# q and k of the last batch transposed by DMA instead of by TensorE, loads of batches 2 and 3 gated four deep, and a new order of issue

## The chip, the cores and the metric

The kernel runs on one core of one Trainium2 chip. The metric is the device time of one execution in microseconds (us). A core has TensorE (PE in the profile; its weight loads are PEld), VectorE (DVE), ScalarE (ACT), GpSimd (POOL) and SyncE (SP), each with its own stream of instructions taken in order, and 16 DMA engines. SBUF is the on-chip memory, PSUM the memory that TensorE writes.

## The reference

An attention with a narrow window feeds a mixing layer. Four batches, 8 heads, 768 positions, head size 64; 512 channels.

```python
# attention: q, k, v are (4, 8, 768, 64); n_global = 8, n_local = 96
scores = scale * np.matmul(q, k.transpose(0, 1, 3, 2))
rel = pos[:, None] - pos[None, :]
keep = (pos[None, :] < n_global) | ((rel >= 0) & (rel < n_local))
scores = scores + (-slopes[:, None, None] * dist[None, :, :])[None]
a = softmax(np.where(keep, scores, -1e9))
x = np.matmul(a, v)            # then (batch, position, 512 channels)
# mixing layer
theta = x @ w_theta
zr, zi = x * np.cos(theta), x * np.sin(theta)
y = einsum('ts,bsd->btd', w_tok_r, zr) + einsum('ts,bsd->btd', w_tok_i, zi)
u = x + y
out = u + np.maximum(u @ w_ch, 0.0)
```

## The kernel before

**Tiling.** A batch's 768 positions are six tiles of 128, taken in three groups `g` of two. Because a query sees 96 positions back and the first 8, a group needs score blocks with its own two key tiles and the last one of the group before. The first 8 keys and values are put in place of the first 8 rows of a tile's copy (`kp`, `kg` in `twin`; `vpa`, `vpb` in `vprev`).

**Names.** Each piece of work has a name with the digits batch, group (or tile), part. For a batch `b`: `load` brings q, k (both as bf16, lines 240 to 251) and v from DRAM through GpSimd's queue; `t{b}{g}{i}0` transposes q (`i` = 0) or k (`i` = 1) of a group on TensorE, eight blocks of 128x128, into PSUM (line 425), and `q{b}{g}0` or `k{b}{g}0` copies the result to SBUF, to the tile `qT` or `kk` (line 439). `kk` has room for each key block twice; the second copy is made by `kp` (line 384) and `kg` (line 388). `s{b}{g}{p}` makes the scores of two heads (line 499), `x` their exponentials on ScalarE (line 526), `m` the multiplication with the table of biases (line 534), `v` the product with the values (line 556), `n` the division (lines 567, 569), which fills the tile `x`. `xt` transposes that tile: on TensorE for batches 0 and 1, by a DMA transpose issued from SP for batches 2 and 3 (line 589). `th` multiplies with w_theta (line 601), `cos` and `sin` run on ScalarE (lines 610, 612), `z` multiplies on VectorE (line 622). `mx{b}{tile}{g}` mixes positions (line 644); `u` adds (line 656); `ut` transposes u, from batch 1 on by a DMA transpose issued from SP (line 676, except the very last tile); `ch` multiplies with w_ch (line 688); `o` makes the output tile on VectorE (line 694); `st` stores it from SP (line 704). `ts` and `tx` load ScalarE's tables for sine and for exponentials (lines 733, 713).

**Stages.** While the mixes and channel products of one batch fill TensorE, the attention of the next runs in between; the mixes of a batch need the `z` of all its groups.

**What sets the order.** All instructions are issued in the order of the text `ORDER` (lines 37 to 92), one global list by name; every engine takes its own part of it in that order. A suffix `/ACT` or `/DVE` picks the engine, `+n` puts n filler matmuls before the operation (`fill`, line 142). The numbers that the `add` calls carry (costs, priorities) aren't used here: `Plan.add` (line 23) keeps name, engine and function. Waits between engines follow from which tiles an instruction reads and writes.

**Buffers.** Tiles of a kind share a fixed number of buffers (line 124): a new tile takes one that is free when everything that used its last tile is done. Those that matter here are the output tiles `o` (3), `qT` and `kk` (3 each), `cs`, the pair of cosine and sine (3), and `pa` and `pb`, the PSUM tiles (4 each).

```python
bufs = dict(qk=6, qT=3, kk=3, e=8, x=8, xT=3, zri=5, cs=3, u=4, uT=3, o=3, w_nat=7, pa=4, pb=4)
```

**Loads.** There are 82, numbered in the order of issue: 47 to 64 are batch 2's, 65 to 82 batch 3's. From load 20 on, each has a gate: a copy of one element on GpSimd that reads what load `n - depth` brought (line 234), so that load `n` isn't issued before that one has landed. The depth is `DEPTH1` = 8 up to load 46 and `DEPTH` = 6 from load 47 on.

**The switch.** `trans_qk` holds a second path that the kernel before does not take, since `TQ` is empty: for the groups listed in `TQ` the transposition is one DMA transpose, issued from SP, straight from the loaded tile to `qT` or to every other block of `kk` (lines 398 to 408), without the copy from PSUM.

Of the kernel before, what the change touches and what calls it, by code (L numbers as in the profile page):

```python
# [15 lines left out]
class Plan:  # L16
# [6 lines left out]
    def add(self, name, eng, fn, **_):  # L23
        op = self.ops[name] = SimpleNamespace(name=name, fn=fn, took=next(iter(eng)))
        return op
# [12 lines left out]
zero hw00 hw10 halfpi rel ones2 ones1 hw01 warm0 ones0 hw11 ones5 ones3 ones6 ones4 load1 tiny sid4 sid3 sid7  # L38
sid1 sid0 sid2 load2 sid5 sid6 ident far0 far1 load3 dtab0 dtab1 dtab2 load4 cast00/ACT dtab3 bi0000+1
cast10/DVE etab5 bi0001 t0000 load5 t0010 q000/ACT bi0010 bi0011 k000/DVE load6 etab7 kg000 cast01/DVE etab4  # L40
load7 kp000/DVE t0001+22 cast11/DVE etab1 s001 q001/DVE t0011 load8 etab0 s000 k001/DVE x0000 load9 kg001
x0001 kp001/DVE t0100+14 etab6 bi0020 load10 bi0021 q010/DVE x0010 t0110 x0011 s002 load11 k010/DVE etab2
bi0030 bi0031 s003 kp010/DVE x0020 load12 x0021 vpa00/DVE bi0100+2 x0030 kg010 vpb00/DVE bi0101+1 load13 x0031
s010 etab3 v000 v002 load14 v001 n000 x0100 bi0110 bi0111 vpa01/DVE s011 x0101 load15 vpb01/DVE bi0120 x0110
v003 n002 bi0121 load16 s012 x0111 n003 bi0130 load17 x0120 v010 n001 bi0131 s013 x0121 load18 n010 bi0200
x0130 v012 load19 v011 x0131 n012 t0200 gate20 t0210 n011 q020/ACT load20 v013 k020/DVE xt00 gate21 bi0201
kg020 xc00/ACT bi0210 kp020/DVE load21 bi0211 vpa02/DVE s020+1 n013 s021 gate22 x0200 vpb02/DVE load22 xt01+6
x0201 bi0220 x0210 xc01/DVE v020+1 bi0221 x0211 gate23 n020 bi0230 load23 s022 bi0231 x0220 s023 gate24 tw00
x0230 load24 th001 twc00/DVE x0231 gate25 x0221 v021 load25 v023 n021 ts0 tw10 gate26 v022 load26 twc10/DVE
th000 n023 gate27 tw11 n022 cos000 load27 th010 twc11/DVE sin000 xt02 gate28 cos001 z000 load28 tw01 sin001  # L50
th011 xc02/DVE gate29 cos010 z001 load29 th020 sin010 twc01/DVE gate30 cos011 load30 th021 z010 sin011 gate31
cos020 t1000 load31 z011 tw20 sin020 q100/DVE tw21 cos021 gate32 mx000 z020 load32 twc20/ACT twc21/DVE mx001
gate33 sin021 vpa10/DVE load33 tx1 vpb10/DVE t1010 z021 mx020 gate34 k100/DVE load34 mx002 kp100/DVE gate35
kg100 mx022 load35 u00 gate36 s100 load36 s101 ut00 x1000 mx021 gate37 x1010 uc00/DVE load37 x1001 tw31 x1011
u02 tw30 twc31/ACT gate38 s102 m100 load38 s103 t1100 x1020 m101 x1030 mx010 gate39 q110/DVE x1031 load39
x1021 v100 m103 mx012 twc30/ACT m102 gate40 load40 n100 tw40 v102 twc40/DVE mx011 gate41 n102 load41 t1110 u01
tw41 gate42 v103 k110/DVE load42 twc41/ACT ut01 ut02 v101 kg110 uc02/DVE ch00 uc01/ACT gate43 kp110/DVE load43
vpa11/DVE ch01 n103 gate44 load44 vpb11/DVE s110 n101 t1200 gate45 x1100 o00 load45 ch02 x1101 q120/DVE st00
t1210 gate46 o01 load46 s111 k120/DVE s112 st01 x1110 mx030 gate47 kp120/DVE x1120 load47 o02 mx032 x1121
kg120 gate48 x1111 m110 st02 mx031 load48 m111 s113 gate49 u03 s120 load49 x1130 tw50 m112 tw51 twc50/ACT v110  # L60
gate50 twc51/DVE xt10 load50 x1131 n110 mx040 vpa12/ACT xc10/DVE gate51 mx042 load51 m113 x1200 mx041
vpb12/DVE x1201 gate52 load52 m120 v111 mx050 n111 gate53 load53 u04 s121 v120 x1210 v113 gate54 n120 ut03
load54 x1211 mx052 n113 uc03/ACT gate55 m121 mx051 load55 vpa20/DVE s122 u05 gate56 s123 x1220 ch03 load56
vpb20/DVE x1221 ut04 x1230 gate57 o03 ut05 v121 load57 uc04/ACT v112 n121 th100 st03 uc05/ACT gate58 n112
x1231 load58 ch04 m122 ts1 m123 gate59 xt11 load59 v122 xc11/DVE cos100 v123 th101 gate60 n122 sin100 load60
n123 ch05 cos101 o04 gate61 sin101 xt12 load61 o05 st04 th110 xc12/ACT vpa21/DVE gate62 st05 z100 th111 load62
cos110 z101 sin110 th120 gate63 vpb21/DVE load63 cos111 z110 th121 sin111 gate64 cos120 load64 t2110 z111
sin120 t2010 k210/DVE gate65 cos121 t2200 load65 z120 mx100 k200/ACT kp210/DVE gate66 q220/DVE mx101 sin121
load66 kp200/DVE tx2 t2000 z121 gate67 mx120 kg210 load67 vpa22/DVE q200/DVE mx102 gate68 vpb22/DVE load68
kg200 mx110 u10 gate69 s200 load69 ut10 s201 mx111 x2000 x2001 gate70 x2010 mx121 load70 m200 x2011 v200 m201  # L70
gate71 mx112 load71 n200 s202 u11 gate72 s203 t2100 x2020 load72 x2021 mx122 ut11 q210/DVE x2030 gate73 x2031
m202 t2210 load73 u12 s210 k220/ACT s211 gate74 vpa30/DVE ut12 ch10 load74 vpb30/DVE x2100 kp220/DVE x2101
mx130 gate75 o10 load75 x2110 m210 s212 x2111 st10 mx131 gate76 m203 x2120 load76 m211 x2121 v210 mx132 n210
gate77 load77 m212 v201 s213 n201 ch11 gate78 x2130 load78 kg220 u13 x2131 v202 s220 n202 gate79 ut13 v203
load79 mx140 x2200 m213 x2201 n203 s221 gate80 load80 v212 vpa31/DVE x2210 xt20 mx142 m220 x2211 gate81 n212
s222 load81 v220 vpb31/DVE x2220 v213 n220 mx141 gate82 x2221 load82 n213 v211 m222 s223 ch12 n211 x2230 x2231
m221 v222 xt21 mx150 ts2 m223 v221 n222 v223 mx151 n221 n223 th200 o12 xt22 th201 o11 cos200 vpa32/DVE sin200
mx152 st11 u14 cos201 st12 vpb32/DVE ch13 sin201 ut14 u15 z200 th210 ut15 o13 th211 cos210 z201 sin210 st13
th221 cos211 z210 t3000 sin211 t3010 q300/DVE t3110 k300/DVE t3210 th220 k310/DVE k320/ACT kp300/DVE t3100
z211 cos220 mx200 kg300 q310/DVE sin220 mx201 cos221 kg310 kp310/DVE kg320 sin221 kp320/DVE t3200 z220 tx3  # L80
ch15 q320/DVE z221 s300 s301 mx220 x3000 o15 x3001 x3010 mx202 st15 m300 x3011 s302 m301 s303 mx222 u20 x3020
x3021 x3030 ut20 v300 m302 mx221 x3031 n300 v302 m303 ch14 n302 s310 o14 s311 x3100 mx210 u22 st14 x3110 v303
x3111 ut22 mx212 n303 x3101 m311 mx211 m310 v301 ch20 u21 n301 ut21 mx230 o20 s312 st20 s313 x3120 mx232 xt30
x3130 v310 x3121 ch22 n310 x3131 m312 s320 s321 o22 x3200 mx250 x3201 m313 st22 v311 x3210 mx231 n311 x3211
m320 s322 s323 u23 x3220 mx251 x3221 m321 ut23 v313 x3230 ch21 m322 x3231 n313 ts3 v312 v321 m323 mx240 n312
v320 o21 v322 xt31 mx241 n320 n321 v323 mx242 st21 n323 n322 th300 u24 xt32 mx252 cos300 sin300 th301 u25 ut24
z300 ch23 cos301 ut25 sin301 th310 o23 z301 th311 st23 cos310 sin310 mx300 cos311 z310 th320 sin311 z311 th321
cos320 sin320 mx301 cos321 z320 ch24 sin321 z321 mx310 o24 mx302 st24 mx311 u30 mx312 ut30 ch25 u31 mx320 ut31
o25 mx322 st25 mx321 ch30 u32 mx330 ut32 o30 mx331 st30 mx332 ch31 u33 mx340 ut33 o31 mx342 st31 mx341 ch32
u34 mx350 ut34 o32 mx351 st32 mx352 ch33 u35 ut35 o33 ch34 uc35/ACT st33 ch35 o34 ch351 o35 st34 o351 st35  # L90
st351
# [4 lines left out]
def kernel(  # L96
# [13 lines left out]
    nc = tc.nc  # L110
# [18 lines left out]
    add = plan.add  # L129
# [33 lines left out]
    TQ = ()  # L163
    TQ_AFTER = None
    DEPTH = 6
# [37 lines left out]
    add("dtab0", {"DVE": 0.34},  # L203
        lambda: nc.vector.tensor_tensor(dtab[:, 0:2], rel, far, op=ALU.add),
        reads=["far"], writes=["dtab"], prio=-6)
    add("dtab1", {"DVE": 0.11}, lambda: nc.vector.tensor_copy(out=dtab[:, 2], in_=dtab[:, 0]),
        reads=["dtab"], writes=["dtab"], prio=-6)
    add("dtab2", {"DVE": 0.14},
        lambda: nc.vector.tensor_scalar(dtab[0:NG, 0:2], dtab[0:NG, 0:2], float(NL), None, op0=ALU.min),
        reads=["dtab"], writes=["dtab"], prio=-6)  # L210
    add("dtab3", {"DVE": 0.14}, lambda: nc.vector.tensor_copy(out=dtab[:, 3:5], in_=dtab[:, 1:3]),
# [66 lines left out]
    def first(i, t):  # L278
# [18 lines left out]
        o = add(f"cast{i}{t}", {"DVE": 0.34, "ACT": 0.49}, cast, reads=[st], writes=[key, key + (i, t)],  # L297
# [77 lines left out]
    def twin(dst, mine, b, g, u0, n):  # L375
# [5 lines left out]

        def copy():
            d_ = tiles[dst][:, :, pr] if halves else tiles[dst][:, u0:u0 + n]
            vector[oc.took](out=d_[:, :, :, 1, NG:T], in_=d_[:, :, :, 0, NG:T])  # L384

        oc = add(f"kp{b}{g}{u0}", {"DVE": dve_t(512 * n, 4), "ACT": act_t(512 * n)}, copy, reads=mine, writes=[dst] + w2)
        add(f"kg{b}{g}{u0}", {"DVE": 0.1},
            lambda: nc.vector.tensor_copy(
                out=tiles[dst][:, td, kd, 1, 0:NG],
                in_=tiles["kk", b, 0][:, 0:1, kd, 0, 0:NG].to_broadcast([T, td.stop - td.start, kd.stop - kd.start, NG])),  # L390
            reads=mine + first_k, writes=[dst] + w2, boost=boost(b, 3))

    def trans_qk(b, g, i, ts):
# [404 lines left out]
```

The softmax here doesn't subtract the row's maximum and nothing guards it: scores larger than these inputs give would overflow.

## Time and profile before

| what | value |
|---|---|
| time, median of 3 runs | 171.06 us (171.0 to 171.14) |
| the profiled execution's time | 171.41 us |
| its span, first to last instruction | 169.6 us |
| GpSimd, busy until | 87 us of the span |
| DMA queue of the loads: 16 engines' share | 96.4% |
| DMA queue of SP: 16 engines' share | 23.4% |

Busy time of the engines in four stretches of the span: the start, until TensorE is without stops; to the end of batch 2's scores; the change to batch 3; the rest until the last products.

```text
us from:to     length    PE     DVE    ACT    POOL
5.30:14.90       9.60   9.00    8.24   8.61    9.60
14.90:97.70     82.80  81.86   73.89  61.35   66.56
97.70:116.00    18.30  18.14   17.05  13.40    0.00
116.00:165.00   49.00  48.36   31.24  18.67    0.00
```

A row of the page's groups reads: line, engine, operation, output tile <- input tiles, shapes, count | busy us, mean ns of one | idle us of the engine just before them, and what ended that idle time. In the chain of waits and in the timeline a row is start in us, length in us, engine, and line. Mean durations of matmuls include their latency in the pipeline; how fast they follow one another is read from the chain, which merges a run of them into one row with its length and count.

### The profile page before, as it was taken

How to read it: one execution, taken by the hardware profiler on the slowest of the kernel's cores; microseconds unless marked ns; L12 is line 12 of the kernel's file. 1: busy time of each engine (PE TensorE's matmuls, PEld its weight loads, DVE VectorE, ACT ScalarE, POOL GpSimd, SP SyncE). 2: the span in 40 equal slices, each digit the busy share in tenths (PEclk: the TensorE clock that was granted, in tenths of full speed). 3: DMA queues.
4: the chain of work that ended last, by engine and by line, in shares of the span. 5: the costliest groups of instructions: out<-in, count | busy, mean ns of one | idle time of the engine just before them, and what ended most of it. 6: DMA issues, size and time to landing. Idle time of an engine off the chain costs nothing.

```text
span 169.6 us, 4122 instructions
## 1 busy us (share of the span) xinstructions
PE 162.1 (96%) x1581; PEld 91.9 (54%) x1608; DVE 136.0 (80%) x316; ACT 103.9 (61%) x186; POOL 80.7 (48%) x150
## 2 busy tenths in 40 slices
PE   7999999999999999999999999999999999999990
PEld 2665756656655656565555554754545644444440
DVE  7888987896999999998699999898859965634442
ACT  3799989986454939994695666695448557200010
POOL 8998689969989989999950000000000000000000
PEclk9999999999999999999999999999999999999999
DMA  4999999999999999999999438303363373143334
GB/s 134 208 155 155 197 191 177 190 178 178 162 164 197 197 143 137 164 221 141 135 156 139 93 66 216 93 0 97 93 126 98 74 173 97 62 108 108 95 97 182
DMA packets 94820, 23.73 MB, mean 140 GB/s; under 512 B 86992, under 2 KB 91856, under 8 KB 94800
## 3 DMA queue, kind: packets, MB, share of 16 engines
q0 software_dynamic: 73504, 12.33, 96.4%
q1 hardware_dynamic: 20240, 10.62, 23.4%
q10 hardware_dynamic: 1056, 0.52, 1.2%
q8 instruction: 12, 0.20, 0.5%
q14 instruction: 8, 0.07, 0.1%
HBM read 25.69 MB, written 6.29 MB: 189 GB/s over the span
## 4 chain that ended last, share of the span: by engine, by line
PE 87%; DVE 6%; ACT 2%; issue 2%; DVEq 0%
PE pb L644 37%; PE pa L601 12%; PE pb L688 10%; PE pa L499 7%; PE pb L425 5%; PE pa L556 5%; PE pa L490 3%; PE pb L367 2%; PE pb L582 2%; PE pb L556 2%; ACT e L526 1%; PE pb L668 1%; DVE sid L215 1%; ACT etab L742 1%; DVE kk L384 1%
## 5 line engine op out<-in xcount | busy, mean ns | idle before, releaser
L644 PE MATMUL pb<-zri,w_tokT 128*128 128x512 bf16 x273 | 67.6, 379 | 1.0 <-issue 0.3
L526 ACT ACTIVATE e<-pa 128x512 bf16<-128x512 f32 (+1 forms) x96 | 47.2, 568 | 25.1 <-PE pa L499 25.0
L644 PEld LDWEIGHTS <-w_tokT 128*128 128x128 bf16 x288 | 25.9, 98 | 26.7
L656 DVE TENSOR_TENSOR u<-x,pb 128x512 bf16<-128x512 bf16 x24 | 16.4, 683 | 11.1 <-PE pb L644 11.1
L534 DVE TENSOR_TENSOR e<-e,etab 128x1024 bf16<-128x1024 bf16 (+1 forms) x36 | 22.3, 639 | 2.6 <-ACT e L526 2.4
L688 PE MATMUL pb<-w_ch_bf,uT 128*128 128x512 bf16 (+1 forms) x96 | 24.0, 371 | 0.2
L601 PE MATMUL pa<-w_theta_bf,xT 128*128 128x512 bf16 x90 | 22.5, 379 | 0.3
L610 ACT ACTIVATE cs<-pa,halfpi 128x512 bf16<-128x512 f32 x24 | 16.8, 700 | 7.9 <-PE pa L601 7.8
L261 POOL DMA_DIRECT2D vn<-in_v_dram x24 | 21.2, 892 | 0.6 <-DMA qk<-in_q_dram 0.4
L247 POOL DMA_DIRECT2D qk<-in_q_dram x22 | 19.6, 890 | 1.4 <-issue 0.7
L247 POOL DMA_DIRECT2D qk<-in_k_dram x22 | 19.3, 879 | 0.4 <-issue 0.3
L622 DVE TENSOR_TENSOR zri<-x,cs 128x1024 bf16<-128x1024 bf16 x24 | 16.4, 685 | 3.5 <-ACT cs L612 3.5
L556 PEld LDWEIGHTS <-e 128*128 128x128 bf16 x352 | 15.0, 98 | 5.8
L694 DVE SCALAR_TENSOR_TENSOR o<-pb,u 128x512 f32<-128x512 f32 (+1 forms) x25 | 16.3, 663 | 2.3 <-PE pb L688 2.3
L569 DVE TENSOR_TENSOR x<-pa,rec 128x256 bf16<-128x256 f32 x36 | 15.3, 425 | 1.2
L499 PE MATMUL pa<-qT,kk 64*128 64x128 bf16 x352 | 15.9, 218 | 0.3 <-DVE qT L436 0.2
L499 PEld LDWEIGHTS <-kk 64*128 64x128 bf16 x352 | 10.0, 94 | 10.8 <-issue 8.1
L612 ACT ACTIVATE cs<-pa 128x512 bf16<-128x512 f32 x24 | 14.7, 612 | 0.0
L672 ACT COPY uT<-pb 128x512 bf16<-128x512 bf16 x5 | 2.8, 589 | 18.8 <-PE pb L668 18.8
L601 PEld LDWEIGHTS <-xT 128*128 128x128 bf16 x96 | 9.0, 98 | 9.5 <-DVE xT L585 0.2
L688 PEld LDWEIGHTS <-uT 128*128 128x128 bf16 x100 | 8.9, 98 | 8.8 <-ACT uT L672 0.5
L425 PE MATMUL pb<-ident,qk 128*128 128x128 bf16 x176 | 12.5, 219 | 0.1
(76 smaller groups left out, 205.3 us busy)
## 6 DMA issues: line engine op xcount, KB each, us to landing
out_dram<-o SPq DMA_DIRECT2D x23, 256.0 KB, 2.5
vn<-in_v_dram POOLq DMA_DIRECT2D x24, 128.0 KB, 5.6
qk<-in_q_dram POOLq DMA_DIRECT2D x22, 128.0 KB, 5.7
qk<-in_k_dram POOLq DMA_DIRECT2D x22, 128.0 KB, 5.5
w_nat<-in_moe_w_tok_r_dram POOLq DMA_DIRECT2D x6, 192.0 KB, 7.9
w_nat<-in_moe_w_tok_i_dram POOLq DMA_DIRECT2D x6, 192.0 KB, 7.3
e<-in_k_dram ACTq DMA_DIRECT2D x2, 256.0 KB, 5.0
e<-in_q_dram SPq DMA_DIRECT2D x2, 256.0 KB, 4.3
```

What stands on the lines that cost most here:

```text
L247: nc.gpsimd.dma_start(out=tiles[key][:, i, t].rearrange("p (h d) -> p h d", d=D), in_=(q, k)[i][b, :, r0:r0 + T, :].rearrange("h p d -> p ...
L261: nc.gpsimd.dma_start(out=v_bufs[i][:, t, :, 0:D], in_=v[b, :, r0:r0 + T, :].rearrange("h p d -> p h d"))
L425: nc.tensor.transpose(p_[:, t - u0, p], tiles[key][:, i, t, p * T:(p + 1) * T], ident)
L499: nc.tensor.matmul(p_[hh][:, s], lhsT=tiles["kk", b, kg][R, kt, p, r, :], rhs=tiles["qT", b, g][R, qt, p, :], start=not biased, stop=not b ...
L526: nc.scalar.activation(tiles[ek][:, hh, 0:n], tiles[pb[hh]][:, 0:n], AF.Exp, scale=scale)
L534: nc.vector.tensor_mul(e_[:, :, 0:n], e_[:, :, 0:n], etab[:, 2 * p:2 * p + 2, s0:s0 + n])
L556: nc.tensor.matmul(o, lhsT=l_, rhs=r_, start=(i == 0), stop=(i == len(mms) - 1))
L601: nc.tensor.matmul(p_, lhsT=tiles["xT", b, g][:, p, t, :], rhs=w_theta_bf[:, p, :], start=(p == 0), stop=(p == NP - 1))
L610: nc.scalar.activation(tiles[ck][:, 0], tiles[ps], AF.Sin, bias=halfpi)
L622: nc.vector.tensor_mul(tiles[zk][:, t].rearrange("n i (p c) -> n i p c", p=NP), tiles["x", b, g][:, None, :, t, :].to_broadcast([T, 2, NP, ...
L644: nc.tensor.matmul(p_, lhsT=w_tokT[wi][:, 2 * g + t, tt * T:(tt + 1) * T], rhs=tiles["z", b, g][:, t, wi, :], start=(n == 1 and t == 0 and ...
L688: nc.tensor.matmul(p_, lhsT=tiles["uT", b, tt][:, p, :], rhs=w_ch_bf[:, p, i * w:(i + 1) * w], start=(p == 0), stop=(p == NP - 1))
```

## The change

Three things change in what is executed. `TQ` lists the three groups of batch 3, so that its six transpositions of q and k (t3000 to t3210) go out as DMA transposes from SP, and the operations q300, k300, q310, k310, q320 and k320 no longer exist. `DEPTH` goes from 6 to 4. `ORDER` is replaced by another list of the remaining names, with 43 filler matmuls in place of 48 and another engine for some of the copies. The buffers stay as they are.

```diff
@@ -160,9 +159,9 @@
     PV, PT = ("pb", "pa"), "pa"
     U_SLOW = 0.8
     SPLIT0 = 0
-    TQ = ()
+    TQ = ((3, 0), (3, 1), (3, 2))
     TQ_AFTER = None
-    DEPTH = 6
+    DEPTH = 4
     DEPTH1 = 8
...
-    add("dtab0", {"DVE": 0.34},
+    add("dtab0", {"DVE": 0.4},
...
-        oc = add(f"kp{b}{g}{u0}", {"DVE": dve_t(512 * n, 4), "ACT": act_t(512 * n)}, copy, reads=mine, writes=[dst] + w2)
-        add(f"kg{b}{g}{u0}", {"DVE": 0.1},
+        oc = add(f"kp{b}{g}{u0}", {"DVE": dve_t(512 * n, 4) + (0.1 if (b, g) == (0, 0) else 0.02), "ACT": act_t(512 * n)}, copy, reads=mine, writes=[dst] + w2)
+        add(f"kg{b}{g}{u0}", {"DVE": 0.25 if (b, g) == (0, 0) else 0.13},
...
```

The other changed numbers are of this kind too (the planner's costs of dtab, cast and etab). Of the list, the start (old, then new):

```diff
-zero hw00 hw10 halfpi rel ones2 ones1 hw01 warm0 ones0 hw11 ones5 ones3 ones6 ones4 load1 tiny sid4 sid3 sid7
-sid1 sid0 sid2 load2 sid5 sid6 ident far0 far1 load3 dtab0 dtab1 dtab2 load4 cast00/ACT dtab3 bi0000+1
-cast10/DVE etab5 bi0001 t0000 load5 t0010 q000/ACT bi0010 bi0011 k000/DVE load6 etab7 kg000 cast01/DVE etab4
-load7 kp000/DVE t0001+22 cast11/DVE etab1 s001 q001/DVE t0011 load8 etab0 s000 k001/DVE x0000 load9 kg001
-x0001 kp001/DVE t0100+14 etab6 bi0020 load10 bi0021 q010/DVE x0010 t0110 x0011 s002 load11 k010/DVE etab2
...
+hw00 ones6 hw10 ones4 ones1 ones2 halfpi rel ones5 zero hw01 hw11 ones0 ones3 load1 tiny warm0 sid3 far0 far1
+load2 dtab0 dtab1 dtab2 load3 dtab3 ident sid2 etab1 sid7 load4 cast00/DVE etab4 sid0 sid1 t0000 sid5 load5
+sid4 bi0000 cast10/DVE etab3 bi0001 bi0010 bi0011 sid6 q000/DVE t0010 load6 etab2 cast01/DVE k000/ACT
+cast11/DVE load7 t0001+17 etab7 kp000/DVE t0011+3 kg000 q001/ACT load8 k001/DVE s000+2 etab6 s001 kg001 load9
+kp001/DVE x0000 t0100+8 x0001 bi0020 load10 x0010 q010/DVE t0110+4 x0011 bi0021 etab0 load11 s002 k010/DVE
...
+load13 etab5 bi0110 bi0111 s011 load14 x0100 v001 vpa01/DVE v000 x0101 bi0120 vpb01/DVE load15 v002 x0110 n000
...
```

and the change from batch 2 to batch 3:

```diff
...
-s222 load81 v220 vpb31/DVE x2220 v213 n220 mx141 gate82 x2221 load82 n213 v211 m222 s223 ch12 n211 x2230 x2231
-m221 v222 xt21 mx150 ts2 m223 v221 n222 v223 mx151 n221 n223 th200 o12 xt22 th201 o11 cos200 vpa32/DVE sin200
-mx152 st11 u14 cos201 st12 vpb32/DVE ch13 sin201 ut14 u15 z200 th210 ut15 o13 th211 cos210 z201 sin210 st13
-th221 cos211 z210 t3000 sin211 t3010 q300/DVE t3110 k300/DVE t3210 th220 k310/DVE k320/ACT kp300/DVE t3100
-z211 cos220 mx200 kg300 q310/DVE sin220 mx201 cos221 kg310 kp310/DVE kg320 sin221 kp320/DVE t3200 z220 tx3
-ch15 q320/DVE z221 s300 s301 mx220 x3000 o15 x3001 x3010 mx202 st15 m300 x3011 s302 m301 s303 mx222 u20 x3020
...
+load81 s221 u13 s222 x2210 mx142 o11 x2211 ut13 gate82 v220 x2220 load82 u14 v213 ch12 x2221 n220 t3000 n213
+s223 th200 m221 x2230 ut14 x2231 m222 v221 mx150 ts2 m223 xt21 n221 v222 v223 mx151 cos200 n222 t3100 n223
+sin200 mx152 vpa32/DVE vpb32/DVE xt22 th201 u15 o12 ch13 cos201 t3010 z200 sin201 ch14 o13 t3110 z201 o14
+mx200 ut15 th210 t3200 th211 cos210 sin210 mx210 t3210 cos211 z210 sin211 th220 st11 z211 th221 st14 cos220
+st13 sin220 kp300/DVE mx201 st12 kg300 cos221 z220 s300 sin221 mx211 tx3 z221 s301 kp310/DVE mx212 kg310 x3000
+x3001 mx202 u21 x3010 x3011 m300 s302 ut21 s303 m301 ch15 x3020 u20 x3021 x3030 v301 m302 v300 x3031 ut20
...
```

## The prediction

> **What bounds the kernel now.** I read the page first, then the chain of waits in order of time, then the stretch between batch 2 and batch 3 on each engine.
>
> ```profile
> span 169.6 us, 4122 instructions
> PE 162.1 (96%) x1581; PEld 91.9 (54%) x1608; DVE 136.0 (80%) x316; ACT 103.9 (61%) x186; POOL 80.7 (48%) x150
> ...
> PE 87%; DVE 6%; ACT 2%; issue 2%; DVEq 0%
> ...
> L425 PE MATMUL pb<-ident,qk 128*128 128x128 bf16 x176 | 12.5, 219 | 0.1
> ```
>
> TensorE is busy 96% of the span and makes 87% of the chain. So work taken off it shows, and so does every wait put in front of it. The chain around the change:
>
> ```profile
> 97.36 0.33 PE pa L499 x8
> 97.69 0.54 PE pb L688 x2
> ...
> 104.84 2.32 PE pa L601 x10
> 107.16 1.79 PE pb L425 x32
> ...
> 109.81 0.45 PE pb L425 x8
> ...
> 111.98 0.45 PE pb L425 x8
> ...
> 113.29 0.44 PE pa L499 x12
> 113.74 1.83 PE pb L644 x8
> 115.57 0.44 PE pa L499 x12
> ```
>
> The reader is to see two things. The 48 transposes of batch 3 (32, 8 and 8) lie on the chain. And TensorE goes from s223 (ending at 97.69, called T below) to s303 (ending at 116.0) without a stop of note: windows give 18.14 us busy of 18.30.
>
> **The change, part by part.**
>
> *Removed from TensorE:* 48 transposes. 32 took 1.79 us, 56 ns each; 48 x 56 ns = 2.69 us. All lie on the chain: **-2.7 us** (2.5 to 2.8). Their evacuations leave VectorE (five of 0.69) and ScalarE (one of 1.01). I cost that at nothing: the chain runs through TensorE there, and what these engines gain would count only where TensorE waits for them.
>
> *Start.* The new order makes dtab right after the first sid, so the first etab can start near 4 us in place of 5.93, filling the time in which ScalarE waited for its cast.
>
> ```profile
> 5.93 0.74 ACT L742 ACTIVATE etab<-dtab 128x640 bf16<-128x640 bf16 x1 [0.77 <-DVE dtab L211]
> ...
> 10.01 0.87 ACT L526 ACTIVATE e<-pa 128x384 bf16<-128x384 f32 x2 [0.36 <-PE pa L499]
> 10.77 0.74 ACT L742 ACTIVATE etab<-dtab 128x640 bf16<-128x640 bf16 x1
> ...
> 14.99 1.08 ACT L526 ACTIVATE e<-pa 128x512 bf16<-128x512 f32 x2
> ```
>
> Three etabs (10.77, 12.13, 14.24) stood between the first exponentials (10.01) and x0100 (14.99); now two do, worth 0.62, and the first exponential comes about 0.4 sooner: cast10 ends near 6.5, k000 on ScalarE near 7.4, cast01 and cast11 near 8.4, kp000 and kg000 near 9.0, s000 and s001 near 9.6 (an estimate from the durations of these lines). Against it, vpa01 now stands ahead of n000 on VectorE and waits for a value load issued near 7.5; value loads land after 4.6 to 7.2 us (median 5.6), so n000 gains little over its 15.22. I take **-0.6** (0 to -1.1). Five pads fewer (43 for 48) are mostly start filler and count in this. Evacuations that trade VectorE for ScalarE, or back (1.01 against 0.69), cost nothing by the cover of ScalarE's idle time (61% busy, 25.0 us waiting for scores); without it each is 0.3 us.
>
> *Six DMA transposes on SP.* The nearest rows are xT's, of the same 256 KB:
>
> ```profile
> L589 SPq DMA_TRANSPOSE xT<-x x6: 1231/1236/1300, 94.2 to 136.5; - x6
> ...
> DMA to landing us min/median/max: 3.1/3.1/3.4
> ```
>
> t3000 and t3100 go out before xt22. t3010 follows it, lands near T+8, and is wanted by kp300 after T+12. So as producers they are hidden; writing every other block of kk is in no row, and I bound it by uT's slowest landing, 5.6, which still lands by T+11. [...] The row has 8 blocks landed in 3.1 us, so the sum goes by the row.
>
> *What SP's place costs.* Here I see the price of the new order. Output tiles `o` have three buffers (line 124). In the old order a store frees one before a fourth is wanted. In the new order o11, o12, o13 and o14 all come before st11, st14, st13, st12. So o14 on VectorE must take o11's buffer and wait until st11 has landed; and SP takes xt22, t3010, t3110, ut15, t3200, t3210 before st11.
>
> ```profile
> 101.30 1.24 SPq L589 DMA_TRANSPOSE xT<-x  x1
> 102.59 1.05 SPq L704 DMA_DIRECT2D out_dram<-o  x2
> ```
>
> xt22 leaves when n223 is done, now at 101.30 = T+3.6. One transpose on SP takes 1.29 to the next issue. Six of them: st11 issues at T+3.6 + 6 x 1.29 = T+11.35. Stores in quiet stretches land after 1.9 to 3.4; I take 2.6, behind transposes: T+13.95. Then o14 (0.61 from one VectorE start to the next), z210 and z211 (0.61 each): T+15.8, with 0.1 for hand-overs T+15.9. Behind o14 on VectorE stand z210, z211, kp300, kg300; mx201 on TensorE waits for z211, and cos221 for a cs buffer that z210 frees.
>
> TensorE meanwhile has th200, v221, mx150, v222, v223, mx151, mx152, th201, ch13, ch14, mx200, th210, th211, mx210, th220, th221: thirteen of 0.86 and three of 0.24 = 11.9 us. One smaller stop lies in it: o13 now stands ahead of z201 on VectorE, so z201 ends about T+7.4 while TensorE has reached mx200 at T+6.7: 0.7. Th221 then ends at T+12.6 and mx201 starts at T+15.9: 3.3. Together they are 15.9 - 11.9 = **+4.0**, and whatever delays TensorE before mx201 is inside that sum; the landings make it 3.3 to 4.8. After it s302 needs x3001: from z210's end at T+15.2 two activations (1.2), the table load (1.5) and two exponentials (0.8) give T+18.7, while TensorE has mx201, s300, mx211, s301, mx212, mx202 until T+19.8. So no third stop.
>
> Would the stop also slow TensorE down afterwards? The page's granted clock is full throughout, yet the first matmuls after a start are slow:
>
> ```profile
> L355 PE MATMUL pb<-zero 128*128 128x512 bf16 x8 | 3.6, 631 | 1.2 <-DVE zero L185 1.2
> ```
>
> Eight 512-column matmuls took 3.6 us where eight later ones take 8 x 0.216 = 1.7. If a stop of 3.3 us brought that back, it would be +1.9; no stop in this trace is longer than 0.7, so the bounds are 0 and +1.9. I take 0. [...]
>
> *Loads four deep.* POOL now issues loads of batches 2 and 3 at 1.10 us each (36 from 47.55 to 87.15), and its gates barely wait. Four deep, a load can start once the fourth before it has landed: with landings of 5.0 (their median there) and 0.18 of gate it is 5.2/4 = 1.30 each, 7 us later at the end, so the last lands near 98. vpa32, which reads it, comes on VectorE after n223, at 101.2; vpa30 stands at 86.25 against a landing near 82.5. Nothing waits. The cover is VectorE's own work up to there; landings over 5.3 us use it up. Changed numbers in the planner's `add` calls run nowhere: `Plan.add` keeps name, engine and function.
>
> **The sum.** 169.6 - 2.7 - 0.6 + 4.0 = 170.3 of span. The profiled execution took 171.41, 1.81 over its span: 172.1. It stood 0.35 above the median of the runs, so on their scale **171.8 us**; own range 170.6 to 173.0.
>
> **The rivals.**
>
> *No buffer wait* (chance 0.18): o14 finds a buffer, or SP's order is not as the list reads. For it: nothing in the trace of before shows such a wait. Against: three buffers and four live tiles. Without the 3.3, but with the 0.7: 168.5, faster.
>
> *The wait is there but smaller than what is won* (0.11): st11 lands after 1.9 us in place of 2.6, and the start gives its 1.1 in place of 0.6: 171.8 - 0.7 - 0.5 = 170.6, at the edge of faster.
>
> *The stop cools TensorE* (0.09): up to +1.9 on the forecast, 173.7. For it: the slow first matmuls. Against: they follow a pause that this trace doesn't measure, from before its first instruction.
>
> *Loads come late, and no buffer wait* (0.04): at landings of 5.6, 1.45 us a load, the last lands near 103.7, 2.5 us behind vpa32, which stands ahead of u15, o12 and z200 on VectorE; mx200 would wait for it. It decides from landings of 5.3 on. Price 2.5, so 168.5 + 2.5 = 171.0, no change; with the buffer wait it would hide inside the 4.0. Against: with fewer in flight, landings should shorten.
>
> **How the numbers follow.** Forecast 0.58, rivals 0.18, 0.11, 0.09, 0.04. A measurement of this kernel tells no less than 0.2% (0.34 us) from no change: faster is under 170.7, slower over 171.4. Faster: 0.18, 0.07 of the second rival and 0.01 of the forecast = 0.26. Same: 0.04 of the second, 0.03 of the last and 0.07 of the forecast = 0.14. Slower: the rest, 0.60. The range reaches from just under the first rival to the cooled case: 168.3 to 173.7.
>
> **What would show it.** Right: line 694 waits on the store's DMA near 105 us for some 6 us, z (line 622) late behind it, TensorE idle some 3 us ahead of line 644 about 13 us after s223, SP issuing st11 after its sixth transpose; 128 matmuls at line 425 in place of 176. Wrong: TensorE as dense there as now (then 168.5); 512-column matmuls spaced 0.43 after the stop (clock); idle at 457 (loads); or first exponentials no earlier than 10.0.

## The result, and the profile after

The changed kernel takes 177.76 us (median of three executions, 177.66 to 178.13) against 171.1 us in the same comparison: a ratio of 1.0393, with an interval of 1.0372 to 1.0414. It is **3.9% slower**; 171.8 was forecast. A fourth execution took 236.14 us at a mean granted clock of 0.66 (0.65 in every window from 20 us on); it is left out here, as are below, from medians, ranges and ratios alike, the executions over 1.5% above the fastest of their kernel. The profile after shown here is of the same kernel in the first experiment (176.38 us, span 174.6 us).

First the page of the kernel after: span, busy time of the engines, shares of the chain of waits, and two groups of instructions.

```profile
span 174.6 us, 4030 instructions
PE 161.3 (92%) x1531; PEld 88.2 (51%) x1555; DVE 131.6 (75%) x313; ACT 101.4 (58%) x183; POOL 83.9 (48%) x150
...
PE 75%; DMA 11%; DVE 4%; issue 3%; ACT 2%; POOL 1%; SPq 1%; DVEq 0%; POOLq 0%; ACTq 0%
...
L643 PE MATMUL pb<-zri,w_tokT 128*128 128x512 bf16 x275 | 69.7, 384 | 5.9 <-DVE zri L621 5.0
...
L693 DVE SCALAR_TENSOR_TENSOR o<-pb,u 128x512 f32<-128x512 f32 (+1 forms) x25 | 16.4, 663 | 11.4 <-DMA out_dram<-o 6.4
```

Lines are numbered one lower than before. TensorE does less (161.3 us, with 50 fewer instructions in the records, of which 48 are transposes), but the span grew by 5.0: its share of the chain fell from 87% to 75%, and DMA, in no place of the chain before, has 11%. The mixes (line 643) waited 5.0 us for `z` where they waited for nothing of note before, and `o` (line 693) waited 6.4 us for one store.

The chain of waits after, in order of time (start, length, what), around the change of batches:

```profile
97.72 6.35 DMA vn<-in_v_dram
...
104.16 0.45 DVE vp L456
...
105.66 0.60 DVE o L693
106.26 0.60 DVE zri L621
...
108.11 0.59 PE pb L643 x2
108.70 1.74 PE pa L600 x8
110.44 0.23 SPq L401
...
110.77 1.28 SPq L401
112.05 0.05 issue
112.10 2.29 DMA out_dram<-o
...
114.48 0.69 DVE o L693
115.17 0.61 DVE zri L621
...
115.82 0.59 PE pb L643 x2
```

Where the chain before ran through TensorE, it now goes through three foreign places: the last value load (issued 97.72, landed 104.07), the issue of transposes on SP (to 112.05), and the landing of st11 (to 114.39), for which o14 waits on VectorE, and mx201 behind it on TensorE. VectorE's two waits, for the last load and for st11 (in brackets the idle time ahead and what ended it):

```profile
104.16 0.44 DVE L456 COPY vp<-vn 128x1040 bf16<-128x1040 bf16 x1 [2.54 <-DMA vn<-in_v_dram]
...
114.48 0.69 DVE L693 SCALAR_TENSOR_TENSOR o<-pb,u 128x512 f32<-128x512 f32 x1 [6.43 <-DMA out_dram<-o]
```

The same place in TensorE's own timeline:

```profile
106.91 0.60 PE L643 MATMUL pb<-zri,w_tokT 128*128 128x512 bf16 x2 [1.58 <-DVE zri L621]
108.11 0.59 PE L643 MATMUL pb<-zri,w_tokT 128*128 128x512 bf16 x2 [0.59 <-DVE zri L621]
108.54 1.89 PE L600 MATMUL pa<-w_theta_bf,xT 128*128 128x512 bf16 x8
110.27 1.03 PE L643 MATMUL pb<-zri,w_tokT 128*128 128x512 bf16 x4
111.13 1.89 PE L600 MATMUL pa<-w_theta_bf,xT 128*128 128x512 bf16 x8
115.82 1.20 PE L643 MATMUL pb<-zri,w_tokT 128*128 128x512 bf16 x4 [2.81 <-DVE zri L621]
116.95 0.45 PE L498 MATMUL pa<-qT,kk 64*128 64x128 bf16 x6
```

Two stops, at mx200 (1.58 and 0.59) and at mx201 (2.81). After the second the six score matmuls take 0.45 where they take 0.34 elsewhere. The windows tell why (length; PE, PEld, DVE, ACT, POOL busy; the granted clock; DMA share; GB/s):

```profile
97.94:116.00 18.06, 12.79 (x80) 5.68 (x78) 8.95 (x20) 8.34 (x15) 0.65 (x1) 1.00 1.06 164
116.00:122.00 6.00, 5.77 (x33) 2.02 (x34) 3.31 (x9) 4.13 (x8) 0.00 (x0) 0.72 0.34 131
122.00:169.00 47.00, 46.47 (x352) 22.96 (x353) 31.39 (x66) 18.39 (x35) 0.00 (x0) 1.00 0.40 105
```

In windows of 1 us the clock is at 1.0 up to 117.0, at 0.5 from there to 120.5, and at 1.0 again. A mean of 0.72 over 6 us is then 0.28 x 2 x 6 = 3.4 us at half clock. The kernel's other executions have only their mean clock on record: of the seven, this one among them, four have 0.981 in place of 0.990, which by the same working would be some 6.7 us at half, an estimate. They took 177.7 to 178.6 us; the three at 0.990 took 176.4 to 178.1. So the clock goes with the longer times, but is not all that sets them apart.

**Where the 5.0 us went.** To add it up, each matmul's start was taken from the trace, and the work ahead of it, each instruction at its undisturbed spacing, was taken off. What is left is the delay up to that point; a step in it is a loss.

| where | kernel before, us | after, us | difference added |
|---|---|---|---|
| delay at 100 us | 9.47 | 9.28 | -0.2 |
| just ahead of mx200 | 9.47 | 9.92 | +0.6 |
| after the stops at mx200 | 9.47 | 12.42 | +2.5 |
| after the stop at mx201 | 9.47 | 15.39 | +3.0 |
| at s302, after the half clock | 9.61 | 17.27 | +1.7 |
| at the end | 10.31 | 18.15 | +0.2 |
| work itself (transposes, fillers) | 155.33 | 152.31 | -3.0 |

The sum is +4.8 of the 5.0; the rest is behind the last matmul.

### The profile page after: what moved, and what is told of

The parts are those of the page before. It is cut to its first block, busy times and chain, and to the rows that moved or that the text cites. A ratio compares the mean times of both kernels' runs of the same rounds, so it can differ in the third digit from the quotient of the medians.

```text
span 234.4 us, 4030 instructions
## 1 busy us (share of the span) xinstructions
PE 225.6 (96%) x1531; PEld 110.6 (47%) x1555; DVE 135.5 (58%) x313; ACT 103.2 (44%) x183; POOL 81.4 (35%) x150
## 4 chain that ended last, share of the span: by engine, by line
PE 94%; DMA 2%; issue 1%; DVE 1%; ACT 1%
PE pb L643 39%; PE pa L600 13%; PE pb L687 13%; PE pa L498 7%; PE pa L555 5%; PE pb L424 4%; PE pa L489 3%; PE pb L366 3%; PE pb L555 2%; PE pb L581 2%; DMA e<-in_q_dram 2%; PE pb L144 1%; PE pb L667 1%; ACT e L525 1%; PE pb L417 0%
## 5 line engine op out<-in xcount | busy, mean ns | idle before, releaser
L643 PE MATMUL pb<-zri,w_tokT 128*128 128x512 bf16 x275 | 98.9, 512 | 1.7 <-issue 0.6
L643 PEld LDWEIGHTS <-w_tokT 128*128 128x128 bf16 x288 | 32.2, 119 | 46.8 <-issue 45.3
L687 PE MATMUL pb<-w_ch_bf,uT 128*128 128x512 bf16 (+1 forms) x94 | 33.3, 495 | 0.9 <-issue 0.3
L600 PE MATMUL pa<-w_theta_bf,xT 128*128 128x512 bf16 x93 | 33.4, 509 | 0.4 <-issue 0.2
L555 PEld LDWEIGHTS <-e 128*128 128x128 bf16 x352 | 18.4, 109 | 9.5 <-issue 6.9
L498 PEld LDWEIGHTS <-kk 64*128 64x128 bf16 x352 | 10.9, 99 | 17.9 <-issue 15.0
L498 PE MATMUL pa<-qT,kk 64*128 64x128 bf16 x352 | 18.8, 240 | 0.1
L600 PEld LDWEIGHTS <-xT 128*128 128x128 bf16 x96 | 10.7, 117 | 16.5 <-issue 15.6
L687 PEld LDWEIGHTS <-uT 128*128 128x128 bf16 x100 | 10.8, 117 | 13.9 <-issue 13.2
L555 PE MATMUL pa<-vn,e 128*128 128x65 bf16 x144 | 14.5, 216 | 0.0
```

What stands on the lines that cost most here:

```text
L498: nc.tensor.matmul(p_[hh][:, s], lhsT=tiles["kk", b, kg][R, kt, p, r, :], rhs=tiles["qT", b, g][R, qt, p, :], start=not biased, stop=not b ...
L555: nc.tensor.matmul(o, lhsT=l_, rhs=r_, start=(i == 0), stop=(i == len(mms) - 1))
L600: nc.tensor.matmul(p_, lhsT=tiles["xT", b, g][:, p, t, :], rhs=w_theta_bf[:, p, :], start=(p == 0), stop=(p == NP - 1))
L643: nc.tensor.matmul(p_, lhsT=w_tokT[wi][:, 2 * g + t, tt * T:(tt + 1) * T], rhs=tiles["z", b, g][:, t, wi, :], start=(n == 1 and t == 0 and ...
L687: nc.tensor.matmul(p_, lhsT=tiles["uT", b, tt][:, p, :], rhs=w_ch_bf[:, p, i * w:(i + 1) * w], start=(p == 0), stop=(p == NP - 1))
```

## The experiments

**1. The change as it is.** No edit; it gave the profile above.

> The changed kernel as it is, for a profile at the clock of the timed runs. Time 177.5 to 178.3 in every theory. Theory A (the wait for an output buffer, then a cooled TensorE): line 693 starts some 6 us late at o14, TensorE stands idle 3 to 4 us ahead of line 643 about 13 us after s223, and matmuls of 512 columns follow one another at 0.43 us in place of 0.216 for several us after it. Theory B (the price lies elsewhere in the new order, the start above all): TensorE stands idle in the first 20 us or while batches 1 and 2 run, by 5 us or more. Theory C (loads four deep come late): idle time of VectorE or TensorE ended by a load's landing.

Measured: 177.56 us (176.38 to 178.59), ratio 1.0395 (1.0358 to 1.0432). Theories A and C both have their sign: every step of the buffer wait is there, and with it two things that were costed at nothing, VectorE's 2.54 us for the last value load and the fall of the clock. Theory B has none: TensorE's delay at 100 us is no larger than before (9.28 against 9.47).

**2. One store moved.** The changed kernel with st11 ahead of the transposes:

```diff
-o11 x2211 ut13 gate82 v220
+o11 x2211 ut13 st11 gate82 v220
...
-th220 st11 z211
+th220 z211
```

> The changed kernel with one store moved: st11 goes out from SP right after ut13, ahead of the six transposes, so that o14 finds a free buffer. Theory A: 168 to 170 us, the whole price is gone and TensorE is dense from T to s303. Theory B: 175 to 178, the store's place matters little. Theory C: 175 to 178 as well.

Measured: 171.43 us (eight of ten executions, 170.88 to 173.19), ratio 1.003 (0.9999 to 1.0062). The waits that TensorE has left in the profile after the start (line, releaser, us in total, times, longest):

```profile
PE pa L600 <- DVE rec L566: 0.6, 1, 0.6
PE pb L687 <- DMA uT<-u: 0.3, 1, 0.3
PE pa L498 <- DVE x L568: 0.2, 1, 0.2
PE pb L643 <- issue: 0.2, 1, 0.2
PE pb L687 <- issue: 0.2, 1, 0.2
```

No mix waits for `z`, and the clock stays at 1.0. One name moved in the list, and nothing else, gives back 6.1 us (177.56 to 171.43). Theories B and C fall. But theory A's 168 to 170 us was missed as well: the kernel is only as fast as the one before, and the transposes saved are paid for again elsewhere.

**3. Six deep again.** The changed kernel with the old depth:

```diff
-    DEPTH = 4
+    DEPTH = 6
```

> The changed kernel with the loads of batches 2 and 3 gated six deep as before. Theory A and theory B: 177.5 to 178.3, no change beyond 0.3%. Theory C: 172 to 175.

Measured: 176.82 and 178.82 us (two of four executions; the other two were longer still), ratio 1.039 (1.032 to 1.0461): nothing gained, though the wait for the last load is gone, so theory C's 172 to 175 falls. TensorE's timeline shows what came in its place:

```profile
86.56 1.04 PE L687 MATMUL pb<-w_ch_bf,uT 128*128 128x512 bf16 x4 [2.14 <-DMA uT<-u]
...
108.43 0.59 PE L643 MATMUL pb<-zri,w_tokT 128*128 128x512 bf16 x2 [0.16 <-DVE zri L621]
...
117.47 1.01 PE L643 MATMUL pb<-zri,w_tokT 128*128 128x512 bf16 x2 [4.13 <-DVE zri L621]
```

The stop at mx200 shrank from 2.17 to 0.16, and the one at mx201 grew from 2.81 to 4.13, because st11 comes when SP gets to it. A new one of 2.14 us appeared at ch10: it asks for its transposed `u` while loads six deep are still running, and that transpose landed after 7.1 us (median 2.4). The clock was at half for 6.8 us, from 116.3, in the stop at mx201, on (windows: 0.52 over 116 to 123).

**4. Four deep in the kernel before.** The reverse, on the old order, without DMA transposes of q and k:

```diff
-    DEPTH = 6
+    DEPTH = 4
```

> The kernel before with its loads of batches 2 and 3 gated four deep and nothing else. Theory A and theory B: 170.9 to 171.4, no change. Theory C: slower by 2 us or more, with waits for loads.

Measured: 172.5 us (nine of ten executions, 171.3 to 173.77), ratio 1.0068 (1.0041 to 1.0096): a loss of some 1.2 us by itself (0.7 to 1.6), more than theories A and B allowed and less than C's 2. VectorE's timeline has a wait that the kernel before does not have:

```profile
104.83 0.44 DVE L457 COPY vp<-vn 128x1040 bf16<-128x1040 bf16 x1 [2.11 <-DMA vn<-in_v_dram]
```

The last load went out at 98.60 in place of 86.22, and vpa32 waited 2.11 us for it even in the old order.

**5. The DMA transposes alone.** The kernel before (its order, six deep), with `TQ` on, the six q and k copies taken out, and the transposes put among the old list's stores and transposes:

```diff
-    TQ = ()
+    TQ = ((3, 0), (3, 1), (3, 2))
...
-m221 v222 xt21 mx150 ts2
+m221 v222 xt21 t3000 mx150 ts2
...
-th200 o12 xt22 th201
+th200 o12 xt22 t3010 th201
...
-z200 th210 ut15 o13 th211 cos210 z201 sin210 st13
+z200 th210 ut15 t3110 t3100 o13 th211 cos210 z201 sin210 st13 t3200 t3210
...
```

> The kernel before with the six DMA transposes alone: old order and six-deep loads, t3000 put behind xt21, t3010 behind xt22, the other four behind ut15 and st13, the twin copies of groups 1 and 2 a little later, and every store ahead of the output tile that needs its buffer. Theory A (the transposes are worth their TensorE time, and the price of the change lies in the store's place and what it triggers): 168.0 to 169.3 us, TensorE without a stop over 0.5 us between batch 2 and batch 3. Rival (the DMA transposes hold up xt22, ut14 or ut15 on SP, or their data comes late for kp300): 170.5 us or more, with TensorE waiting for th220, ch15 or s300.

Measured: **169.15 us** (168.77 to 169.43), ratio 0.9891 (0.9878 to 0.9904), faster than both kernels. SP's timeline (a column of starts, one of lengths):

```profile
100.90 1.79 SPq L588 DMA_TRANSPOSE xT<-x  x1
102.86 1.24 SPq L401 DMA_TRANSPOSE kk<-qk  x1
104.19 1.03 SPq L703 DMA_DIRECT2D out_dram<-o  x2
105.32 2.54 SPq L675 DMA_TRANSPOSE uT<-u  x2
```

Two stores (st11 and st12) go out at 104.19, where st11 went out at 112.10 in the changed kernel, and no wait of TensorE is left in the view of waits from 14 us on. Theory A's range is met, and its rival falls. So the replacement of TensorE's transposes does most of what its price said: worth 1.9 us on the medians (171.0 to 169.15) where 2.7 was the price of the instructions.

**6. Store moved and six deep.** Experiments 2 and 3 together.

> The changed kernel with st11 moved up as in e2 and the loads six deep again. Theory D (loads four deep come late for vpa32, near 104 us, and slow SP's transposes there): 169 to 170.5 us, no wait of VectorE for a load, TensorE's idle time between 95 and 106 us gone. Rival (four deep is what keeps batch 1's DMA transposes of u fast, as the 2.3 us stop ahead of ch10 with six deep suggests): 171.5 to 173 us, that stop stays and takes back what is won.

Measured: 171.16 us (nine of twelve executions, 170.53 to 171.68; 171.38 over all twelve), ratio 1.0003 (0.999 to 1.0016): no change from the kernel before. No wait of VectorE for a load is left, yet theory D's 169 to 170.5 is missed; the wait at ch10 is 1.3 us here, as the rival had it, and the time lies just under the rival's range. With the store in its place, neither depth wins.

**7. Fillers ahead of mx201.** The changed kernel with 16 matmuls in the place of the stop, to keep TensorE busy; the wait itself stays:

```diff
-kp300/DVE mx201 st12
+kp300/DVE mx201+16 st12
```

> The changed kernel with 16 filler matmuls of 512 columns (zeros added into the same sum) ahead of mx201, so that TensorE works while VectorE waits for the output buffer. Same wait, no idle TensorE. If the stop cools TensorE's clock, the stretch at half clock goes away: 174 to 176 us. If the clock costs nothing: 177.5 us, or up to 0.5 more.

Measured: 176.76 us (five of six executions, 175.76 to 178.0), ratio 1.0328 (1.0292 to 1.0364). TensorE's timeline:

```profile
113.10 3.62 PE L146 MATMUL pb<-zero 128*128 128x512 bf16 x16
117.90 1.20 PE L643 MATMUL pb<-zri,w_tokT 128*128 128x512 bf16 x4 [1.18 <-DVE zri L621]
119.03 0.34 PE L498 MATMUL pa<-qT,kk 64*128 64x128 bf16 x6
```

The score matmuls behind it take 0.34 again, and the clock is 1.0 in all windows from 110 to 125. From there to s302 the delay grows by 0.5 us, where it grew by 1.9 in experiment 1. So the half clock cost about 1.4 us in such an execution, by two executions set side by side. The times do not show it clearly: the medians differ by 0.8 us (177.56 and 176.76, from two comparisons), the intervals of the two ratios overlap, and 176.76 lies above the 174 to 176 expected. In the execution profiled st11 left at 114.06, 2.0 later than in experiment 1; TensorE had come to this stretch 1.2 us later (th200 at 98.82 against 97.66), and SP took 2.82 us over t3100 (2.22 there).

**8. A fourth output buffer.** The changed kernel, its list untouched, with the wait taken away by room (x gives up a buffer for it):

```diff
-x=8, xT=3, zri=5, cs=3, u=4, uT=3, o=3,
+x=7, xT=3, zri=5, cs=3, u=4, uT=3, o=4,
```

> The changed kernel with four buffers for the output tiles in place of three (and seven for x in place of eight, to make room; the list of work untouched, so st11 still stands behind six transposes on SP). Theory (o14 stood for the one buffer that st11 had to free, and what the late store cost came through that wait alone): line 693 no longer waits on a store, TensorE has no stop of 3 us at mx201 and no half clock after it, and the time is that of the kernel with st11 moved, 171.6 us (171.0 to 172.5). Rival (SP's late places are the cost by themselves, or VectorE is late from the last load's wait of 2.5 us at line 456): a stop of 2 us or more stays ahead of mx200 or mx201, and the time stays above 174.

Measured: 171.26 us (eight of twelve executions, 170.8 to 172.88), ratio 1.0021 (0.9993 to 1.005). That is the time of experiment 2 by another way. The other four took 174.0 to 176.2 us, and the profile fell on one of them (175.77 us). In it no wait of line 693 for a store is left, so the price of st11's place came through the one buffer; but the wait for the last load (2.90 us at line 456) still stops TensorE at mx200, as the rival had it. What makes the four long is not shown beyond this one profile; the last section comes back to it.

**9. ch10 asked for later.** Experiment 6 with ch10, o10 and st10 moved back:

```diff
-x2030 ch10 n200
+x2030 n200
...
-mx122 x2110
+mx122 ch10 o10 x2110
...
```

> The changed kernel with st11 after ut13 and loads six deep, as in the run at 171.38 us, with ch10 and o10 moved behind mx122 and st10 behind mx130, so that TensorE asks for the transposed u of tile 10 some 2 us later. Theory (of the 2.6 us that the new order still loses with the store in its place, 1.3 to 1.5 is ch10's wait for a DMA transpose that lands after 6 us while loads run): the stop ahead of ch10 near 84 us goes, and the time is 170.1 us (169.6 to 170.6). Rival (something after it is as late, so that what is won there is waited for again): the stop goes, but the time stays at 171.4 within 0.3.

Measured: 170.96 us (170.74 to 172.01), ratio 0.9989 (0.9974 to 1.0004). The stop at ch10 is gone from the timeline, but of its 1.3 us only 0.2 shows in the time (170.96 after 171.16, from two comparisons whose intervals overlap): a miss for the theory, and nearer to the rival's 171.1 to 171.7. At 100 us the delay is 11.06 in place of 11.30 in experiment 6.

**10. The new start on experiment 5.** The new list up to n000, then the list of experiment 5.

```diff
-zero hw00 hw10 halfpi rel ones2 ones1 hw01 warm0 ones0 hw11 ones5 ones3 ones6 ones4 load1 tiny sid4 sid3 sid7
+hw00 ones6 hw10 ones4 ones1 ones2 halfpi rel ones5 zero hw01 hw11 ones0 ones3 load1 tiny warm0 sid3 far0 far1
...
```

> The new order's start up to n000 (dtab and the first etabs early, 31 fillers), then the old order with the six DMA transposes as in the run at 169.15 us, loads six deep. Theory (the start is worth 0.4 to 0.5 us, seen at 15 and 30 us of the changed kernel, and nothing later takes it back): 168.7 us (168.4 to 168.9). Rival (the loads, a steady 1.1 us each, set the pace of batches 1 and 2, so that the start is waited away by 60 us): 169.15 within 0.2.

Measured: **168.2 us** (168.04 to 168.73), ratio 0.9832 (0.9812 to 0.9851), the best of all. ScalarE's first exponentials:

```profile
9.70 1.64 ACT L524 ACTIVATE e<-pa 128x384 bf16<-128x384 f32 x4 [0.29 <-PE pa L497]
11.20 0.76 ACT L740 ACTIVATE etab<-dtab 128x640 bf16<-128x640 bf16 x1
```

They start at 9.70 in place of 10.01, and x0100 at 14.26 in place of 14.99. On the medians the start is worth 0.95 us, more than the theory's 0.4 to 0.5; the intervals of the two ratios don't overlap, so the rival's 169.15 falls. The two profiled executions do not show it at their end: this one (168.73) is the longest of its kernel and that of experiment 5 (168.77) the shortest of its own, and in them the lead is 0.77 us at mx100 (74.06 against 74.83) and 0.13 at mx200 (107.10 against 107.23). How much of the 0.95 is the start, and how much scatter between the two comparisons, stays open.

## Why the prediction was wrong

The direction and its mechanism were right; the time lay outside the range. The term for the stops was too small, because SP got to xt22 later than counted; the start was given too much; and the fall of TensorE's clock and the wait for the last load were set to nothing.

- **The transposes removed, -2.7.** Right. 128 matmuls are left at line 424, and the work of TensorE fell by 3.0 us with five fillers fewer. Experiment 5 keeps 1.9 of the 2.7 on the medians.
- **The start, -0.6.** The first exponentials came at 9.69 and x0100 at 14.25, 0.74 earlier; at 30 us TensorE's delay is 0.49 smaller. By 100 us only 0.2 of it was left in the changed kernel, since other places of the new order gave it back.
- **Three output buffers, and o14 behind st11.** Right, and shown from two sides: moving the store (experiment 2) or adding a buffer (experiment 8) takes the time to 171.4 and 171.3. The rival without that wait falls with the 6.43 us at line 693.
- **Its size, +4.0.** This is the term that was mis-sized: the stops measured 2.5 + 3.0 = 5.5, and 0.6 in small ones ahead of them. The failed step is "xt22 leaves when n223 is done, now at 101.30 = T+3.6". It left at 103.88, which is T+5.9 with T at 97.94, because SP was not free. The timeline of SP after:

```profile
97.19 1.26 SPq L401 DMA_TRANSPOSE qT<-qk  x1
98.56 1.41 SPq L675 DMA_TRANSPOSE uT<-u  x1
100.02 1.37 SPq L588 DMA_TRANSPOSE xT<-x  x1
101.57 2.22 SPq L401 DMA_TRANSPOSE qT<-qk  x1
103.88 1.27 SPq L588 DMA_TRANSPOSE xT<-x  x1
105.25 2.69 SPq L401 DMA_TRANSPOSE kk<-qk  x2
```

SP issues back to back from 97.19 on: t3000 and t3100, which the prediction put "before xt22" without counting their time, take slots of their own, and t3100 took 2.22 us where 1.24 was counted. From xt22 on the forecast nearly holds: six slots in 8.22 us (7.74 forecast), landing in 2.29 (2.6 forecast). One step went the other way: "mx201 on TensorE waits for z211" is 0.6 too late, since its first two products need z210 alone and began behind it (115.17 + 0.61). So mx201 started at 115.82 = T+17.9, where T+15.9 was forecast.
- **The stop at mx200, 0.7.** Measured 2.17 of idle time. The failed step is "Nothing waits", said of the loads four deep. The forecast had the loads at 1.30 us each, the last landed near 98. They went at 1.38 (49.51 to 97.72), began 2.0 later than before, and the last landed after 6.35: at 104.07. vpa32 stood ready at 101.6 and waited 2.54, close to the 2.5 that the rival of late loads gave, at a chance of 0.04. Experiment 4 shows it apart from the rest: some 1.2 us in the kernel before. In the changed kernel it hides behind the store, as the prediction held: SP issued without a gap over 0.2 us from 97.19 to st11 at 112.10, so vpa32's wait did not move st11, which released mx201. Experiment 3 agrees in part: without the wait the stop at mx200 is 2.0 shorter and that at mx201 1.3 longer, but ch10's new wait lies ahead of both.
- **Cooling, 0.** "I take 0" failed, though its rival had been priced right: half clock for 3.4 us in the execution profiled, and, estimated from their mean clock, for 6.7 in four others. The delay grew by 1.9 between mx201 and s302, the upper bound given; in the profile of experiment 7, with TensorE kept busy, it grew by 0.5. The stop measured 2.81 us (3.0 by delay); behind its first matmul TensorE waits for no more than 0.2 us at a time in the trace of before, so that trace could not show what follows such a stop.
- **What the sum left out.** With the store in its place, the new order still runs 2.6 us later at the end than the kernel before, work aside (12.9 against 10.3). The delays put 0.5 of it at ch10, 1.1 between 95 and 100 us and the rest behind 100. Experiment 9 took the first away and won little by it. What causes the others was not tested and stays open.

By the forecast's own scale: 170.3 of span, less 0.3 for the fillers and transposes, plus 0.4 of the start not kept, plus 2.1 of stops, 1.7 of half clock, and 0.4 behind it and at the end, is 174.6. That is the execution profiled, the shortest of the seven; their median, 177.76 us, is 1.4 longer, and no profile shows where.

## What to carry to other kernels

Price a wait behind a queue by the time at which the queue gets to it, with every instruction ahead of it since the queue was last free, and not from the moment at which its input is ready. When work goes over to a transfer, move the small instructions that share the queue first: here one store, moved, was worth 6.1 us, over twice what the removed matmuls cost. And when a forecast opens a stop on TensorE longer than any in the trace, price a half clock behind it in the likeliest sum; here, behind a stop of 2.81 us, it was some 1.4 to 1.9 us.

## What the runs showed of the hardware

**Half clock after stops of TensorE.** In experiment 1, after the stop of 2.81 us, it began at 117.0, 1.2 us after TensorE was at work again, and lasted 3.4; in experiment 3, with the stop of 4.13, it began within the stop, at 116.3, and lasted 6.8. It came with two shorter stops close together too. In the execution of experiment 8 that was profiled, TensorE stood 1.75 us, did two matmuls, and stood 0.59:

```profile
109.19 0.61 PE L643 MATMUL pb<-zri,w_tokT 128*128 128x512 bf16 x2 [1.75 <-DVE zri L621]
110.39 1.01 PE L643 MATMUL pb<-zri,w_tokT 128*128 128x512 bf16 x2 [0.59 <-DVE zri L621]
111.19 1.06 PE L600 MATMUL pa<-w_theta_bf,xT 128*128 128x512 bf16 x2
```

and the windows of that execution have the clock at half for 3.3 us:

```profile
105.00:110.00 5.00, 2.62 (x11) 0.76 (x10) 3.53 (x7) 1.17 (x2) 0.00 (x0) 0.99 0.93 184
110.00:113.30 3.30, 2.91 (x7) 0.99 (x7) 0.94 (x2) 0.16 (x1) 0.00 (x0) 0.50 0.79 151
113.30:120.00 6.70, 6.65 (x40) 2.90 (x40) 3.58 (x8) 6.13 (x12) 0.00 (x0) 1.00 0.75 220
```

In experiment 1 stops of 1.58 and 0.59 at the same place left it at 1.0. Which length of a stop is enough, and what sets how long the half clock lasts, is not shown. It is one execution of each kernel, and no more is claimed from it.

**DMA transposes from SP landed later while loads ran.** In the kernel before, the transposes of `u` issued between 80 and 87 us, with loads under way, landed after 4.8 to 5.6 us; the next one, issued at 92.43 when the last load had landed (91.5), after 2.41. In experiment 3 one took 7.1 with loads running. Loads are not the whole of it: in experiment 3, whose loads had all landed by 92.1, two transposes that SP issued at 102.43 and 103.91, back to back with others, still landed after 4.6 and 4.1. Nor do they explain the long issue of t3100 (2.22 us in experiment 1, 2.82 in experiment 7): with the loads landed by 92.2 it took 1.31 in experiment 3 and 2.37 in experiment 6. Its cause stays open. Writing every other block of `kk` did not make them land later: in experiment 1 those transposes took 3.1 to 3.5 us to land, those of xT before 3.1 to 3.4.
